# Turns of q' in the rounded 4-byte format from copies elsewhere in SBUF, two reads of x in other places, and 128-row rest products

## The chip, the cores and the metric

One NeuronCore of one Trainium2 chip runs the whole program. The metric is the device time of one launch in microseconds (us), the median of the runs shown. Engines are named as in the profile: PE (TensorE matmul), PEld (its weight load), DVE (VectorE), ACT (ScalarE), POOL (GpSimd), SP (SyncE). SP and POOL issue nearly all DMAs.

## The reference, cut to what matters

With x of shape [1, 2048, 576], 32 heads of 18 columns, and phi(t) = where(t > 0, t + 1, exp(t)) + 1e-6:

```python
q, k, v = heads(x @ wqkv)
kv  = einsum("bhsd,bhse->bhde", phi(k), v);  z = einsum("bhsd->bhd", phi(k))
num = einsum("bhqd,bhde->bhqe", phi(q), kv)
den = einsum("bhqd,bhd->bhq", phi(q), z)[..., None] + 1e-6
a = merge_heads(num / den) @ wo                                  # linear attention
fa = einsum("bsd,ed->bse", x, dft_hid_re);  fb = einsum("bsd,ed->bse", x, dft_hid_im)
b = einsum("ts,bse->bte", dft_seq_re, fa) - einsum("ts,bse->bte", dft_seq_im, fb)
g = sigmoid((x * gate_w).sum(-1, keepdims=True))
out = g * a + (1 - g) * b
```

All of it is float32. All DFT matrices come in as inputs.

## The kernel before, in words

The 2048 rows are 16 tiles of 128 rows (`NT`), or 8 pairs of tiles. The 576 columns are 4 blocks of 128 and a rest of 64 (`REST`), and for products two halves of 288 (`HALF`). Nearly all products run on operands of the type `R` (float32r, the rounded 4-byte format; `F` is plain float32): a value is split by ACT into a rounded `hi` (`hi_of`) and by DVE into `lo` = value minus `hi` (`lo_of`), and a product is the sum of three matmuls, hi·hi, hi·lo and lo·hi.

The stages, by time in the profile:

- 5 to 64 us: k' = phi(x Wk) for all 16 tiles, kept in `acc` and split into `pk`.
- 64 to 134 us: xᵀk' (matmuls `bank<-pk,c`), from it the head blocks of kv (`kv_step`, matmuls `bank<-gt,plain` on 252, 126, 144 and 72 columns), and the sums z.
- 134 to 196 us, the q' stage: q' = phi(x Wq) tile by tile (`q_tile`), 14 matmuls for each half; the second half has two more columns that give the gate. q' is written over `acc`. Beside it `build_kv` and `build_m` form the matrix M of 576 x 576 (kv of all heads times wo), which POOL's DMAs move into place (`move_m`) and `split_m` splits into `mw`. `normalise` on DVE divides each tile of q' by its denominators, in steps of a generator called `norms`.
- 185 to 258 us, the q'M stage: for each pair of tiles, `transposed` turns the normalised q': on PE 8 transposes of 128 x 128 out of `acc` (line 826) and one of the two rests of 64 columns, which DVE had copied to `last` (line 827), all with an identity matrix `ident` as the moving operand, in plain float32. ACT and DVE split the turned tiles into `qs`. Then 28 matmuls for each tile (line 226, `bank<-mw,qs`) give the attention output; ACT scales it with the gate and POOL's DMA stores it to DRAM (`att<-acc`). The turns of pair k stand ahead of the products of tile 2k-1.
- 258 to 310 us and 485 to 537 us, the hidden stages: x times the real, then the imaginary hidden DFT matrix, by seven products of quarter blocks (Strassen and Winograd's scheme). For each of 8 row pairs (p) and seven products (k) there are six matmuls on 128 rows (`bank<-wf,xf` or `bank<-wf,xb`) and one, the rest product, on 96 rows that hold the remaining 32 columns of each quarter three times, for hi·lo, hi·hi and lo·hi (line 1012, `bank<-wf,xr`, 56 in each of the two stages). The sums of x (`xforms`, tile name `xm`; `xrest`, `xr`) and of the weights (`wm`, by `right`) are made on DVE and ACT beside the stages before, written to DRAM scratch by POOL's DMAs (class `Left`, function `right`) and read back by SP's DMAs (`load_x`, `load_w`, `load_rest`). Pairs 0 and 1 of x are used straight from SBUF in the first hidden stage, pair 7 (`seven`) is written early.
- 310 to 485 us and 537 to 716 us, the sequence stages: the sequence DFT matrices times those results, again by seven products (line 1171).

ACT, DVE and SP run in the order in which the code is written. On PE the order up to the end of the q' stage is set by a scheduler, and from the q'M stage on by the code. POOL's order is the scheduler's. SBUF is laid out by hand, by offsets such as `T_AT + 76544`: buffers share places over time, and a transfer into a place waits for the last use of what lay there. `Ring` gives a few places in turn. The tables `early` (for the q' stage) and `plan` (for the q'M stage) say at which tile a step of a generator is called.

Of the kernel before, what the change touches and what calls it, by code (L numbers as in the profile page):

```python
# [8 lines left out]
F = mybir.dt.float32  # L9
# [133 lines left out]
def kernel(  # L143
# [111 lines left out]
    ident = const([P, P], F, "ident")  # L255
    make_identity(nc, ident)
# [142 lines left out]
    xrest = scratch([NP * 96, 7 * P], "xr")  # L399
    xrest_of = xrest.rearrange("(g q j r) n -> g j r q n", g=2, q=4, j=3)  # L400
# [54 lines left out]
    def right(src, rest, order):  # L455

        main, last = scratch([P, 7, 2, 2, HALF], "wm"), scratch([96, 7, HALF], "wm")

        def load(k, start):
            c = at(start, [P, 7, 2, HALF], R, "wb")[:P if k < 2 else 96]  # L460
            r, raw = c.bitcast(F)[:, :, 1], src[k] if k < 2 else rest
            for a, b in ((slice(0, 3), slice(0, 3)), (5, 3)):
                begin_after(nc.gpsimd.dma_start(out=r[:, a], in_=raw[:, b]), done[-1])
            return c

        def piece(k, start):

            c = load(k, start)
            r = c.bitcast(F)[:, :, 1]
            yield  # L470
# [4 lines left out]
            add(r[:, 6], r[:, 4], r[:, 1], ALU.subtract)  # L475
            yield
            hi_of(c[:, :, 0], r)
            yield
            if k < 2:
                for fs in (slice(0, 4), slice(4, 7)):  # L480
                    lo_of(c[:, fs, 1], r[:, fs], c[:, fs, 0])
                    nc.gpsimd.dma_start(out=main[:, fs, k], in_=c.bitcast(F)[:, fs])
                    if fs.start == 0:
                        yield
            else:
                rows = slice(32, 64)
                lo_of(c[rows, :, 0], r[rows], c[rows, :, 0])
                yield
                nc.gpsimd.dma_start(out=last, in_=c.bitcast(F)[:, :, 0])

        return (main, last), [piece(*o) for o in order]
# [127 lines left out]
    def xg_next(lo_of=lo_of):  # L619
        if xg_raw:  # L620
# [4 lines left out]
            else:  # L625
# [4 lines left out]
                                              (2, T_AT + 76544)))  # L630
# [145 lines left out]
    def q_tile(i):  # L776
        xs = kept.pop(0) if i < KEPT else split.pop(0)
        for h in range(2):
            ps = bank()[:, :QH[h]]
            run(ps, steps(xs, lambda j: wqt.row(h, j)))  # L780
# [10 lines left out]
    def normalise(k):  # L791
# [10 lines left out]
        for i in range(2):  # L802
# [4 lines left out]
            if i == 1:  # L807
                lasts.append(at(last_ring.next(), [P, 2, REST], F, "last"))
                nc.vector.tensor_copy(out=lasts[-1], in_=acc_pairs[k][:, :, KC * P:])
            yield  # L810

    lasts, last_ring = [], Ring(T_AT + 92672, 2 * REST * 4, 3)
# [5 lines left out]
    def transposed(k):  # L818

        both = [at(qs_ring.next(), [P, 9, P], R, "qs") for _ in range(2)]  # L820
        mains = [bank(), bank()]
        last = bank()[:, :P]
        for i in range(2):
            for c in range(KC):
                cs = slice(c * P, (c + 1) * P)
                nc.tensor.transpose(mains[i][:, cs], acc[2 * k + i][:, cs], ident)  # L826
        nc.tensor.transpose(last, lasts.pop(0).rearrange("p a b -> p (a b)"), ident)  # L827
# [3 lines left out]
        for i, t in enumerate(both):  # L831
            mine, other = ((slice(0, REST), slice(REST, P))[j] for j in (i, 1 - i))
            hi_of(t[mine, 8], last[mine])
            lo_of(t[other, 8], last[mine], t[mine, 8])
        return both
# [56 lines left out]
    def split_m(h):  # L892
        hi_of(mhi[:, :KC, h], mraw[:, :, h])
        lo_of(mlo[:, :, h], mraw[:, :, h], mhi[:, :KC, h])
        hi_of(mhi[:, KC, h], mrest[:, h])
# [15 lines left out]
    for f in wo_split:  # L911
        f()
    kv_step(4)
    q_tile(1)
    build_kv()
# [7 lines left out]
    early = {4: [(norms, 2)], 5: [(norms, 1), (wr_pieces[2], 1)],  # L923
             6: [(norms, 1)], 7: [(wr_pieces[2], 1)],
             8: [(wr_pieces[2], 1), (norms, 1)], 9: [(wr_pieces[2], 1), ("seven", 1)],
             10: [("seven", 1)], 11: [(wr_pieces[2], 1)],
             12: [(wr_pieces[2], 1), ("seven", 1)], 14: [("seven", 1), (norms, 1)],
             15: [("seven", 1), (norms, 1)]}
    for i in range(4, NT):
        for part in early.get(i, ()) if i > 12 else ():  # L930
            go(seven if part[0] == "seven" else part[0], part[1])
        q_tile(i)
# [5 lines left out]
        for part in early.get(i, ()) if i < 13 else ():  # L938
            go(seven if part[0] == "seven" else part[0], part[1])
        if i == NT - 3:  # L940
            queue = transposed(0)
        if i in (10, 11):
            split_m(i - 10)
# [26 lines left out]
    class Hidden:  # L970
# [4 lines left out]
        def load_w(self, k):  # L975
# [6 lines left out]
            nc.sync.dma_start(out=rl.bitcast(F)[:96], in_=self.last[:, f])  # L982
            self.w[k] = wl, rl

        def load_rest(self, p):

            self.rest[p] = at(self.lay.rest(p), [P, 7, P], R, "xr")
            n = min(NP * 96 - p * 96, P)
            nc.sync.dma_start(out=self.rest[p].bitcast(F)[:n], in_=xrest[p * 96:p * 96 + n])
# [140 lines left out]
    def sequence(m, g, src, dst, last=None, between=None):  # L1130
# [97 lines left out]
        3: [(0, 1)], 4: [(0, 1)], 5: [(0, 1)], 6: [(0, 1)], 7: [(0, 1)],  # L1228
        11: [(1, 1)], 12: [(1, 1)], 13: [(1, 1)], 14: [(1, 2)],
    }  # L1230
    paced.enter_context(tc.manual_schedule(engines={mybir.EngineType.PE}))
    for i in range(NT):
# [22 lines left out]
        for p, j in ((1, 8), (2, 11), (3, 15)):  # L1255
# [16 lines left out]
    def late(n):  # L1272
# [15 lines left out]
        if n == 31:  # L1288
            second.load_pair(2)
            second.load_rest(2)  # L1290
            second.load_rest(4)
            second.load_pair(3)
            second.load_rest(3)
            mi.load(0)
# [100 lines left out]
```

## Time and profile before

| | us |
|---|---|
| median of 3 runs | 717.15 (716.99 to 717.18) |
| the profiled execution: device time | 717.38 |
| its span, first to last instruction | 715.7 |
| PE busy | 711.6 |
| DVE busy | 601.1 |
| ACT busy | 338.5 |
| POOL busy | 54.9 |

The profiled execution has 1.7 us outside its span. The granted clock of TensorE is 1.0 over the whole run. In the groups of instructions a row reads: line, engine, operation, what is written and read, shapes and count, busy time in us, mean ns of one. The mean ns of a matmul counts from its start to the end of its drain, and matmuls overlap; what one costs in a row of its kind is read from the chain of waits instead, where pieces of one line stand one behind the other in order of time (start, us, line, count).

### The profile page before, as it was taken

The numbers are of one execution on the slowest core, as the hardware profiler recorded it, in microseconds if no ns is written. First come the engines' busy times: TensorE is split into PE (matmuls) and PEld (weight loads), VectorE is DVE, ScalarE is ACT, GpSimd is POOL, SyncE is SP. The second block draws the span as 40 slices with busy tenths as digits, with TensorE's granted clock in tenths as the row PEclk, the third lists the DMA queues.
The fourth block names the chain that finished last, engine by engine and source line by source line (L and its number), as shares of the span: only waits on it lengthen the run. The fifth ranks groups of instructions, "written<-read, shape, count | busy, mean of one in ns | idle before, by whom it ended". The sixth has DMA issues, their size and how long they took to land.

```text
span 715.7 us, 13965 instructions
## 1 busy us (share of the span) xinstructions
PE 711.6 (99%) x5436; PEld 711.1 (99%) x5436; DVE 601.1 (84%) x1020; ACT 338.5 (47%) x587; POOL 54.9 (8%) x94
## 2 busy tenths in 40 slices
PE   9999999999999999999999999999999999999998
PEld 9999999999999999999999999999999999999998
DVE  5699977687999748989999999857889988888885
ACT  5998445677644444553534334323535433343331
POOL 1112200050131110000010000000000000000000
PEclk9999999999999999999999999999999999999999
DMA  7388896874594589753475675789973544454530
GB/s 259 105 280 312 318 303 209 301 213 129 180 368 183 195 307 366 237 184 118 150 257 184 212 254 208 278 312 402 377 260 94 184 132 144 127 181 155 179 131 34
DMA packets 57525, 157.84 MB, mean 221 GB/s; under 512 B 6388, under 2 KB 15668, under 8 KB 56436
## 3 DMA queue, kind: packets, MB, share of 16 engines
q1 hardware_dynamic: 48404, 118.44, 48.9%
q0 software_dynamic: 8768, 38.12, 14.7%
q8 instruction: 43, 0.70, 0.4%
q10 hardware_dynamic: 288, 0.39, 0.2%
q14 instruction: 22, 0.18, 0.1%
HBM read 114.06 MB, written 41.39 MB: 217 GB/s over the span
## 4 chain that ended last, share of the span: by engine, by line
PE 99%; DVE 0%; issue 0%
PE bank L1171 49%; PE bank L226 23%; PE bank L1012 14%; PE bank L725 8%; PE bank L558 2%; PE bank L826 1%; PE bank L252 1%; PE bank L704 0%; PE bank L707 0%; PE bank L827 0%; DVE row L1188 0%
## 5 line engine op out<-in xcount | busy, mean ns | idle before, releaser
L1171 PE MATMUL bank<-fh,c 128*128 128x288 f32 x1792 | 350.7, 293 | 0.0
L1171 PEld LDWEIGHTS bank<-fh,c 128*128 128x128 f32 x1792 | 285.1, 188 | 0.0
L1171 PE MATMUL bank<-fl,c 128*128 128x288 f32 x896 | 262.3, 293 | 0.0
L196 ACT ACTIVATE c<-craw 128x768 fp32r<-128x768 f32 (+2 forms) x148 | 126.9, 900 | 163.6 <-DVE craw L216 154.0
L1171 PEld LDWEIGHTS bank<-fl,c 128*128 128x128 f32 x896 | 168.2, 188 | 0.0
L206 DVE TENSOR_TENSOR c<-craw,c 128x768 fp32r<-128x768 f32 (+3 forms) x148 | 146.1, 1024 | 0.8 <-ACT c L196 0.8
L226 PE MATMUL bank<-wd,xs 128*128 128x288 f32 (+1 forms) x784 | 104.9, 294 | 0.0
L226 PEld LDWEIGHTS bank<-wd,xs 128*128 128x128 f32 x784 | 103.5, 188 | 0.0
L1012 PE MATMUL bank<-wf,xf 128*128 128x288 f32 x588 | 90.8, 294 | 0.0
L1012 PEld LDWEIGHTS bank<-wf,xf 128*128 128x128 f32 x588 | 83.3, 189 | 0.0
L226 PE MATMUL bank<-mw,qs 128*128 128x288 f32 x448 | 60.7, 295 | 0.0
L725 PE MATMUL bank<-pk,c 128*128 128x288 f32 x448 | 60.0, 294 | 0.0
L725 PEld LDWEIGHTS bank<-pk,c 128*128 128x128 f32 x448 | 59.1, 188 | 0.0
L226 PEld LDWEIGHTS bank<-mw,qs 128*128 128x128 f32 x448 | 59.0, 188 | 0.0
L216 DVE TENSOR_TENSOR craw<-craw,craw 128x256 f32<-128x256 f32 x128 | 54.4, 425 | 5.1
L216 DVE TENSOR_TENSOR ys<-bank,ys 128x288 f32<-128x288 f32 x63 | 28.8, 457 | 28.2 <-PE bank L1171 25.7
L216 DVE TENSOR_TENSOR craw<-craw 128x512 f32<-128x512 f32 x64 | 43.9, 687 | 7.6 <-PE bank L1171 3.7
L196 ACT ACTIVATE fh<-fl 128x864 fp32r<-128x864 f32 (+1 forms) x36 | 30.3, 868 | 28.0 <-DVE fl L216 20.0
L395 DVE SCALAR_TENSOR_TENSOR acc<-bank,e 128x288 f32<-128x288 f32 x64 | 28.6, 454 | 16.5 <-ACT e L394 16.3
L206 DVE TENSOR_TENSOR fl<-fl,fh 128x864 fp32r<-128x864 f32 (+1 forms) x36 | 35.4, 988 | 1.6
L1012 PE MATMUL bank<-wf,xr 96*128 96x288 f32 x112 | 33.3, 298 | 0.0
L216 DVE TENSOR_TENSOR fl<-bank,y 128x288 f32<-128x288 f32 x48 | 21.8, 454 | 11.1 <-PE bank L1012 9.6
(106 smaller groups left out, 662.1 us busy)
## 6 DMA issues: line engine op xcount, KB each, us to landing
xf<-xm SPq DMA_DIRECT2D x42, 512.0 KB, 9.2
craw<-in_cr_dram SPq DMA_DIRECT2D x32, 512.0 KB, 3.9
craw<-in_ci_dram SPq DMA_DIRECT2D x32, 512.0 KB, 3.7
xm<-xb POOLq DMA_DIRECT2D x8, 1024.0 KB, 6.6
wf<-wm SPq DMA_DIRECT2D x14, 576.0 KB, 6.4
xraw<-in_xa_dram SPq DMA_DIRECT2D x25, 320.0 KB, 3.5
xr<-xr SPq DMA_DIRECT2D x14, 448.0 KB, 8.5
xm<-xb POOLq DMA_DIRECT2D x8, 768.0 KB, 8.2
```

What stands on the lines that cost most here:

```text
L196: return nc.scalar.activation(dst, src, AF.Copy, bias=bias)
L206: nc.vector.tensor_tensor(out=dst, in0=src, in1=hi, op=ALU.subtract)
L216: nc.vector.tensor_tensor(out=dst, in0=a, in1=b, op=op)
L226: nc.tensor.matmul(ps, a, b, start=(n == 0), stop=(n == len(pairs) - 1))
L252: nc.tensor.matmul(warm[:, :136], unit[:, :P], unit, start=True, stop=True)
L395: nc.vector.scalar_tensor_tensor(dst, ps, 0.0, e, op0=ALU.max, op1=ALU.add)
L558: nc.tensor.matmul(ps[i][h], x[:, i_x * P:(i_x + 1) * P], wkt.row(h, j), start=(c == 0 and n == 0), stop=(c == KC and n == 1))
L725: nc.tensor.matmul(ps[h][:, :HALF], t[:, a, k], pk[s][:, b, half(h)], start=(s == 0 and n == 0), stop=(s == NT - 1 and n == len(turn) - 1))
L826: nc.tensor.transpose(mains[i][:, cs], acc[2 * k + i][:, cs], ident)
L1012: nc.tensor.matmul(ps, a, b, start=(start and n == 0), stop=(n == len(ops) - 1), skip_group_check=True)
L1171: nc.tensor.matmul(ps[q], c[x][l > 2][:, l - 3 * (l > 2), k], factors[p](y, f), start=(p == 0 and i == 0), stop=(p == NP - 1 and i == 2))
```

## The change

Seven things change.

1. `ident` is now in the type `R`: POOL builds it in plain float32 as `unit_f`, and one ACT instruction copies it. The normalised pair of q' is copied by two POOL DMAs, bit by bit, from `acc` and `last` to one of three buffers `turn` of type `R` (`move_normal`), and `turn` transposes out of these instead of `acc`. Number and shape of the transposes stay: 72 of 128 x 128.
2. `norms` and the small pieces are called at other tiles (`early`, `plan`): the normalisation of pairs 3 to 7 ends one tile sooner than before, that of pair 1 two, that of pair 2 six.
3. `q_tile` opens both halves at once: 9 matmuls of the first half, 9 of the second, then 5 and 5. The turns of pair 0 stand between the 9s and the 5s of tile 13. PE follows the written order from tile 2 of the q' stage on.
4. The last 32 rows of the rest products are filled with zeros: `last` of the weights and `xr` have 128 rows, and a rest product is a matmul on 128 rows. `rest_piece` makes the rest of the weights on 64 partitions of half the width, with a zeroed third part (POOL's memset) and 8 DMAs to DRAM instead of one, and zeros behind the last pair of `xrest`.
5. The rest piece of the weights lies at `T_AT + 84672` instead of `T_AT + 76544`, `last` at `T_AT + 63232`. Pair 2 of x is read into `T_AT + 65536` to `T_AT + 79872`.
6. Pair 2 of x is read at tile 0 of the q'M stage instead of 3, pair 3 at tiles 9 to 12, one piece at a time, instead of 15. Before the second hidden stage the rest of pair 4 is read behind pair 3 instead of ahead of it.
7. `split_m` is cut into `m_hi` (tiles 9 and 10) and `m_lo` (tiles 10 and 11).

```diff
-    ident = const([P, P], F, "ident")
-    make_identity(nc, ident)
+    unit_f = at(SLOT_AT + P * 4, [P, P], F, "unit_f")
+    make_identity(nc, unit_f)
+    ident = const([P, P], R, "ident")
+    nc.scalar.activation(ident, unit_f, AF.Copy)
...
-    xrest = scratch([NP * 96, 7 * P], "xr")
+    xrest = scratch([NP * 96 + 32, 7 * P], "xr")
...
-        main, last = scratch([P, 7, 2, 2, HALF], "wm"), scratch([96, 7, HALF], "wm")
+        main, last = scratch([P, 7, 2, 2, HALF], "wm"), scratch([P, 7, HALF], "wm")
...
+        def rest_piece(start):
+            c = at(start, [2 * 32, 3, 7, HALF // 2], R, "wb")
+            f = c.bitcast(F)
+            r = f[:, 1]
+            load(r, rest)
+            nc.gpsimd.memset(f[:, 2], 0.0)
+            yield
+            for _ in sums(r):
+                pass
+            yield
+            hi_of(c[:, 0], r)
+            yield
+            lo_of(c[:, 1], r, c[:, 0])
+            for k, a in enumerate((0, 1, 0, 2)):
+                for q in range(2):
+                    ps, cs = slice(q * 32, q * 32 + 32), slice(q * HALF // 2, (q + 1) * HALF // 2)
+                    nc.gpsimd.dma_start(out=last[k * 32:k * 32 + 32, :, cs], in_=f[ps, a])
...
     wr_forms, wr_pieces = right(wr, wr_rest, ((0, ACC_AT + 6144), (1, T_AT + 113664),
-                                              (2, T_AT + 76544)))
+                                              (2, T_AT + 84672)))
...
-    def q_tile(i):
+    def q_tile(i, between=iter(())):
...
+        both = [bank()[:, :QH[h]] for h in range(2)]
+        todo = [list(steps(xs, lambda j, h=h: wqt.row(h, j))) for h in range(2)]
+        for part in (slice(0, 9), slice(9, 14)):
+            for h in range(2):
+                for n in range(part.start, part.stop):
+                    nc.tensor.matmul(both[h], *todo[h][n], start=(n == 0), stop=(n == 13))
+            if part.start == 0:
+                next(between, None)
...
+    def move_normal():
+        while normal:
+            k, last = normal.pop(0)
+            o = turn_ring.next()
+            main = at(o, [P, 2, KC * P], R, "turn")
+            rest = at(o + 2 * KC * P * 4, [P, 2, REST], R, "turn")
+            nc.gpsimd.dma_start(out=main.bitcast(F), in_=acc_pairs[k][:, :, :KC * P])
+            nc.gpsimd.dma_start(out=rest.bitcast(F), in_=last)
+            moved.append((main, rest))
...
-                nc.tensor.transpose(mains[i][:, cs], acc[2 * k + i][:, cs], ident)
-        nc.tensor.transpose(last, lasts.pop(0).rearrange("p a b -> p (a b)"), ident)
+                nc.tensor.transpose(mains[i][:, cs].bitcast(R), main[:, i, cs], ident)
+        nc.tensor.transpose(last.bitcast(R), rest.rearrange("p a b -> p (a b)"), ident)
+        yield
...
-    early = {4: [(norms, 2)], 5: [(norms, 1), (wr_pieces[2], 1)],
...
+    early = {4: [(norms, 2), (wr_pieces[2], 1)], 5: [(norms, 1)],
...
+        move_normal()
         if i == NT - 3:
-            queue = transposed(0)
+            go(turning)
...
-            nc.sync.dma_start(out=rl.bitcast(F)[:96], in_=self.last[:, f])
+            nc.sync.dma_start(out=rl.bitcast(F), in_=self.last[:, f])
...
-            ops.append((self.rest[p][:96, 6 - k], wl[:96]))
+            ops.append((self.rest[p][:, 6 - k], wl))
...
-        3: [(0, 1)], 4: [(0, 1)], 5: [(0, 1)], 6: [(0, 1)], 7: [(0, 1)],
+        2: [(0, 1)], 3: [(0, 1)], 5: [(0, 1)], 10: [(0, 1)], 11: [(0, 1), (1, 1)],
...
-        go(norms, 1 if i in (4, 6) else 2)
+        go(norms, 1 if i in (2, 4) else 2)
         for k, n in plan.get(i, ()):
             go(made[k], n)
+        move_normal()
...
-        if i == 3:
+        if i == 0:
             hidden.load_pair(2)
-        if i == 15:
-            hidden.load_pair(3)
+        for k, j in ((0, 9), (2, 10), (4, 11), (6, 12)):
+            if i == j:
+                hidden.load_x(3, k)
```

How the order of instructions moves at the places that the prediction speaks of. On PE, at tile 13 of the q' stage (`wd` is a half of Wq, `xs` a tile of x, split; `acc_87` is pair 0 of q'), before:

```order
L226 MATMUL bank<-wd_1308,xs_2303 128x290
L226 MATMUL bank<-wd_1307,xs_2303 128x290
L826 MATMUL bank<-ident_76,acc_87 128x128 x4
L226 MATMUL bank<-wd_1424,xs_2303 128x288 x5
L226 MATMUL bank<-wd_1307,xs_2303 128x290 x5
L826 MATMUL bank<-ident_76,acc_87 128x128 x4
L827 MATMUL bank<-ident_76,last_2043 128x128
L226 MATMUL bank<-wd_1424,xs_2350 128x288
```

The same place now (line 803 is in `q_tile`, 868 and 869 in `turn`):

```order
L803 MATMUL bank<-wd_1309,xs_2334 128x290
L868 MATMUL bank<-ident_81,turn_2057 128x128 x8
L869 MATMUL bank<-ident_81,turn_2058 128x128
L803 MATMUL bank<-wd_1426,xs_2334 128x288 x5
L803 MATMUL bank<-wd_1309,xs_2334 128x290 x5
L803 MATMUL bank<-wd_1426,xs_2385 128x288
```

The nine transposes stand together and read `turn`, no longer `acc`. In the q'M stage they stand at the same places as before.

On POOL, tiles 0 to 4 of the q'M stage, before (`att` is the store of a tile's attention output, `xb` the quarters of x pairs 0 and 1 read in):

```order
L1241 DMA att_2620<-acc_87 128x576
L411 DMA xb_2665<-in_xq_dram 128x2x256 x2
L1241 DMA att_2621<-acc_87 128x576
L1241 DMA att_2622<-acc_88 128x576
L1241 DMA att_2623<-acc_88 128x576
L411 DMA xb_2834<-in_xq_dram 128x2x256 x2
L1241 DMA att_2608<-acc_89 128x576
```

The same place now:

```order
L1297 DMA att_2651<-acc_89 128x576
L413 DMA xb_2695<-in_xq_dram 128x2x256 x2
L1297 DMA att_2652<-acc_89 128x576
L850 DMA turn_2768<-acc_92 128x2x512
L851 DMA turn_2769<-last_2766 128x128
L1297 DMA att_2653<-acc_90 128x576
L1297 DMA att_2654<-acc_90 128x576
L413 DMA xb_2874<-in_xq_dram 128x2x256 x2
L1297 DMA att_2639<-acc_91 128x576
L850 DMA turn_2914<-acc_93 128x2x512
L851 DMA turn_2915<-last_2912 128x128
```

The copies of pair 3 (`acc_92`) stand behind the store of tile 1, and those of pair 4 (`acc_93`) behind the store of tile 4; pairs 5, 6 and 7 follow behind tiles 6, 8 and 10. The copies of pairs 0 to 2 are issued in the q' stage.

On SP, the reads of x pair 3 for the first hidden stage, before (`xm_98` is pair 3; `wf` are weights, `xr` rests of x):

```order
L981 DMA wf_3412<-wm_359 128x4x288
L982 DMA wf_3413<-wm_360 96x288
L989 DMA xr_3449<-xr_103 128x896
L995 DMA xf_3451<-xm_98 128x1024
L995 DMA xf_3453<-xm_98 128x1024
L995 DMA xf_3455<-xm_98 128x1024
L995 DMA xf_3457<-xm_98 128x512
L989 DMA xr_3479<-xr_103 128x896
```

And now (`xm_100` is pair 3):

```order
L1052 DMA xf_3212<-xm_100 128x1024
L1039 DMA wf_3259<-wm_361 128x4x288
L1040 DMA wf_3260<-wm_362 128x288
L1052 DMA xf_3263<-xm_100 128x1024
L1052 DMA xf_3324<-xm_100 128x1024
L1039 DMA wf_3361<-wm_361 128x4x288
L1040 DMA wf_3362<-wm_362 128x288
L1052 DMA xf_3365<-xm_100 128x512
```

The four reads of pair 3 stand between the reads of weights, ahead of the last one. The reads of pair 2 stand right behind the last tile of x for q' both before and now; what differs for them is the place they are written to, which the rest piece of the weights no longer overlaps.

More of the change, by code (lines that the diff above doesn't have):

```diff
@@ L475, in piece @@
             add(r[:, 6], r[:, 4], r[:, 1], ALU.subtract)
+        def piece(k, start):
+            c = at(start, [P, 7, 2, HALF], R, "wb")
+            r = c.bitcast(F)[:, :, 1]
+            load(r, src[k])
+            yield
+            yield from sums(r)
             yield
@@ L834, in transposed @@
             lo_of(t[other, 8], last[mine], t[mine, 8])
+    def transposed(k):
+        both = []
+        for _ in turn(k, both):
+            pass
         return both
@@ L931 @@
             go(seven if part[0] == "seven" else part[0], part[1])
-        q_tile(i)
+        if i == NT - 3:
+            queue = []
+            turning = turn(0, queue)
+            q_tile(i, turning)
+        else:
+            q_tile(i)
         build_m({4: (2, 3), 5: (4,)}.get(i, ()))
```

85 lines of the change are left out of this document (41 added, 44 removed).

## The prediction

> **What bounds the kernel now.** I read the totals first, then the chain that ended last, then PE's waits, then PE's groups by shape. Totals and chain, from the page:
>
> ```profile
> PE 711.6 (99%) x5436; PEld 711.1 (99%) x5436; DVE 601.1 (84%) x1020; ACT 338.5 (47%) x587; POOL 54.9 (8%) x94
> PE 99%; DVE 0%; issue 0%
> PE bank L1171 49%; PE bank L226 23%; PE bank L1012 14%; PE bank L725 8%; PE bank L558 2%; PE bank L826 1%; PE bank L252 1%; PE bank L704 0%; PE bank L707 0%; PE bank L827 0%; DVE row L1188 0%
> ```
>
> The waits of PE, one row in all (waited for: us, times, longest):
>
> ```profile
> PE bank L252 <- PEq L1382: 0.8, 1, 0.8
> ```
>
> PE waits once, 0.8 us, at the very start. From there to the end its instructions are the chain, one behind the other. So the kernel gets shorter only where an instruction on PE gets shorter or goes, and longer where PE meets a wait that it does not have today. Everything else in this change (DVE, ACT, POOL, SP, DMA) counts by the second of these alone.
>
> Now what the touched instructions cost. The chain of waits in order of time (start, us, line, count), first where rounded matmuls of 252 and 126 (then 144 and 72) columns alternate in `kv_step`, then where turns stand among the products of q'M:
>
> ```profile
> 134.01 0.11 PE bank L704
> 134.12 0.06 PE bank L707
> 134.18 0.17 PE bank L704
> 134.35 0.06 PE bank L707
> 134.41 0.07 PE bank L704
> 134.48 0.04 PE bank L707
> ...
> 196.50 0.87 PE bank L826 x8
> 197.38 0.11 PE bank L827
> ...
> 205.75 7.34 PE bank L226 x56
> ...
> 221.42 0.87 PE bank L826 x8
> ```
>
> Eight transposes take 0.87 us, 109 ns each, and the ninth 0.11. A product of 288 columns takes 7.34 / 56 = 131 ns. So 128 columns in plain float32 cost 0.85 ns a column, 288 rounded ones 0.45. A rounded matmul of 126 columns (line 707) holds the chain for 0.06 us; but with its neighbour of 252 columns it is 0.17 + 0.06 = 0.23 us, 0.115 for each of two weight loads.
>
> The groups by shape, matmuls and then weight loads (count | busy, mean ns):
>
> ```profile
> L1012 PE MATMUL bank<-wf,xf 128*128 128x288 f32 x588 | 90.8, 294 | 0.0
> L1012 PE MATMUL bank<-wf,xr 96*128 96x288 f32 x112 | 33.3, 298 | 0.0
> L826 PE MATMUL bank<-ident,acc 128*128 128x128 f32 x64 | 8.4, 272 | 0.0
> L827 PE MATMUL bank<-ident,last 128*128 128x128 f32 x8 | 2.2, 273 | 0.0
> L226 PEld LDWEIGHTS bank<-mw,qs 128*128 128x128 f32 x448 | 59.0, 188 | 0.0
> L826 PEld LDWEIGHTS bank<-ident,acc 128*128 128x128 f32 x64 | 7.5, 140 | 0.0
> L707 PEld LDWEIGHTS bank<-gt,plain 128*126 128x126 f32 x20 | 3.8, 189 | 0.0
> L704 PEld LDWEIGHTS bank<-gt,plain 128*72 128x72 f32 x5 | 0.7, 141 | 0.0
> ```
>
> The last two columns of mean times matter. A rest product on 96 rows lasts 298 ns, its neighbours on 128 rows 294. A rounded weight load of 126 or 128 columns lasts 188 or 189 ns, one of 72 columns 141; the load of a transpose, though it has 128 columns, lasts 140.
>
> **The turns.** Before: 64 x 0.109 + 8 x 0.11 = 7.9 us. No row shows a rounded transpose. From below the bound is the shortest rounded matmul, 72 columns in 0.04 us: 72 x 0.04 = 2.9 us, a gain of 5.0. From above it is the rounded weight load that binds in `kv_step`, 0.115 us: 72 x 0.115 = 8.3 us, a loss of 0.4. I take 0.06, the row of line 707, as nearest in type and width: 72 x 0.06 = 4.3 us, a gain of 3.6. The reason to take it rather than 0.115 is the weight load: in a turn it already lasts 140 ns instead of 188, as short as a rounded one of 72 columns, and two of those with their matmuls take 0.07 + 0.04 = 0.11 us, 0.055 each. So if the turn's load keeps that length, 0.055 to 0.06 is what both load and columns give.
>
> Here a rule of the Trainium skill speaks against the change. "TensorE: Matmul & The Clock Gate", section "LDWEIGHTS (loading the stationary operand)", gives a weight load's time as its columns over 1.2, so 107 ns for 128 columns, however many rows it has; by it a turn stays at 107 ns, and the estimate is 72 x 0.107 = 7.7 us, a gain of 0.2 instead of 3.6. The alternating row above (0.115 for a load of 126 columns) agrees with it, the shorter load of the transposes does not.
>
> **The rest products.** 112 of them, each 298 - 294 = 4 ns longer than its neighbours: 112 x 4 = 0.45 us gained if 128 rows cost what they cost there. Bounds: nothing, or 0.45. I take 0.45, since the shape becomes that of the neighbours exactly. The reads of weights grow from 96 to 128 rows on SP's queue, off PE's path.
>
> **The copies of q'.** 16 DMAs on POOL's queue, of 512 and 64 KB a pair, and PE now waits for them. Pairs 0 to 2 are copied many tiles ahead. Pair 3 has three tiles, pairs 4 to 7 two tiles between copy and turn. The timeline of POOL shows when the store ahead of pair 4's copies is issued:
>
> ```profile
> 214.04 0.56 POOL L1241 DMA_DIRECT2D att<-acc  x1 [1.57 <-ACT acc L1239]
> ```
>
> What transfers of that queue take, from the DMA issues between 213 and 247 us (count, KB each, median us to landing):
>
> ```profile
> att<-acc POOLq DMA_DIRECT2D x8, 288.0 KB, 2.8
> ...
> xm<-xb POOLq DMA_DIRECT2D x1, 1024.0 KB, 5.9
> xm<-xb POOLq DMA_DIRECT2D x1, 768.0 KB, 3.9
> ```
>
> And from those between 185 and 258.4 us:
>
> ```profile
> xm<-xb POOLq DMA_DIRECT2D x3, 768.0 KB, 9.2
> ```
>
> The copy is issued at about 214.04 + 0.56 = 214.6 and its turn stands at 221.42, or 221.0 once the turn between is 0.4 us shorter: 6.4 us. For 576 KB I go by the quiet rows, between 2.8 for 288 KB and 3.9 for 768: about 3.5 us. That leaves 2.9 us, so I cost the copies at nothing. What hides them is the products of two tiles, 7.34 us; if that cover fails, each us of lateness is a us of PE, up to four times.
>
> DVE must also have normalised the pair by then. Busy times by stretch (PE, PEld, DVE, ACT, POOL, then granted clock, DMA share, GB/s):
>
> ```profile
> 160.00:185.00 25.00, 25.00 (x192) 25.00 (x191) 20.98 (x37) 20.83 (x46) 2.31 (x3) 1.00 0.37 113
> 197.00:213.50 16.50, 16.50 (x132) 16.50 (x131) 15.26 (x30) 7.19 (x18) 5.11 (x8) 1.00 1.02 378
> 213.50:230.00 16.50, 16.50 (x131) 16.50 (x130) 15.14 (x27) 8.49 (x19) 2.74 (x5) 1.00 0.54 197
> ```
>
> DVE has 1.2 to 1.4 us free of 16.5. The change moves work on it between tiles and adds none, and the normalisation ends one tile sooner, which is the tile that the copy takes back.
>
> **The moved reads and the rest.** SP's timeline, last tiles of x for q' and the reads that follow:
>
> ```profile
> 173.32 4.04 SPq L283 DMA_DIRECT2D xraw<-in_xa_dram  x2
> 188.23 1.75 SPq L995 DMA_DIRECT2D xf<-xm  x4
> ...
> 255.92 3.83 SPq L995 DMA_DIRECT2D xf<-xm  x4
> ```
>
> Today pair 2 waits from 177.4 to 188.2 us for the rest piece of the weights, which lies in its place, and then falls into the stretch where the DMA engines are full (share 1.02). With the new places it can start at about 177, in a stretch with a share of 0.37. Pair 3's four reads move from 256 us into the gaps of tiles 9 to 12, behind weights, and ahead of the last weights. PE waits for none of these today, so nothing is gained on its path: 0. They make room for the 4.6 MB of copies.
>
> The ACT copy of `ident` stands ahead of the first split of the weights. ACT's timeline there:
>
> ```profile
> 2.53 0.31 ACT L258 ACTIVATE ones<-ones_f 128x128 fp32r<-128x128 f32 x1
> 4.12 0.44 ACT L196 ACTIVATE wd<-wraw 128x288 fp32r<-128x288 f32 x1 [1.28 <-DMA wraw<-in_wk_dram]
> ```
>
> ACT sits idle for 1.28 us there; another 0.3 us fits: 0. The interleaved halves of `q_tile` are the same 28 matmuls with two banks open instead of one: 0, at most the 0.8 us of one bursting split in the last tile. The rest piece halves the width of its DVE work and adds a memset and 7 DMAs on POOL, which is 8% busy: 0.
>
> **The sum**, against the profiled execution: 717.38 us, of which 715.7 is span and 1.7 lies around it. Span after: 715.7 - 3.6 - 0.45 = 711.65; time 713.3. The median of the runs stands 0.23 below that execution, so 713.1; I say 713.2.
>
> **The rivals.**
>
> *The weight load binds the turn.* For it: 0.115 us for each load in `kv_step`, and rounded loads of 128 columns last 188 ns everywhere. Against it: the turn's load lasts 140. Then a turn costs 0.109 to 0.115, and the rest products are all that is left: 717.15 - 0.45 + (0 to 0.4) = 716.7 to 717.1, within what a measurement here can tell from no change (0.2%, 1.4 us). The rule of the Trainium skill named above would give the same. Chance 0.23.
>
> *The copies land late.* The other side. For it: the row of 768 KB between 185 and 258 us, 9.2 us; with it each of four copies misses its turn by 9.2 - 6.4 = 2.8 us, 11.2 in all: 713.2 + 11.2 = 724.4. Against it: pair 2's reads leave just that stretch, and after 213 us the same transfers take 3.9 and 5.9. It decides slower from 713.2 + 4 x L = 718.6, where L = 1.35 us, so from a landing of 7.75 us. Chance 0.14: 0.09 past that point (718.6 to 724), 0.05 short of it (714 to 718).
>
> *A turn is bound by neither and costs between,* 0.08 us: 717.15 - 2.1 - 0.45 = 714.6. Chance 0.06; the rest, 0.57, is the forecast, with its own range of 711.7 (0.04 us a turn) to 714.2 (0.5 us of small waits and no gain from the rest products).
>
> **How the numbers follow.** Faster by over 0.2%: 0.57 + 0.06 and a little of the late copies, 0.65. Within 0.2%: 0.23 and the rest of the small delays, 0.25. Slower: 0.10. The range runs from 711.7 to 717.4, so that the rival of the weight load with 0.3 us of small waits lies in it; what is left out is late copies past 717.4 and a turn below 0.04 us.
>
> **What would show it.** Right: in the chain of waits nine transposes together take about 0.5 us instead of 0.98; PE has no wait but the first; the group of rest products reads 294 ns. The forecast falls if the transposes keep 109 ns or more; if PE's waits name a DMA of `turn` at one of pairs 4 to 7 (PE would then sit between the products of two tiles); or if at the start of the first hidden stage PE waits for `wf`, whose reads wait for the stores `att` that now share POOL's queue with the copies.

## The result, and the profile after

The changed kernel is slower: 720.87 us (median of 6 runs, 720.69 to 723.44) against 717.16 (6 runs, 716.42 to 717.35), ratio over all runs 1.0063, 95% interval 1.0051 to 1.0074. The forecast was 713.2 with a range up to 717.4. The execution in the profile took 723.44 us, 2.6 more than the median.

The totals of the page, and its chain:

```profile
PE 713.0 (99%) x5436; PEld 712.2 (99%) x5436; DVE 597.3 (83%) x1020; ACT 336.6 (47%) x588; POOL 75.2 (10%) x127
PE 91%; issue 5%; POOL 2%; DMA 1%; DVE 0%; POOLq 0%
```

Before, the chain was PE to 99%. Now POOL, a DMA and issue time stand in it. PE's waits name the DMA (us in all, times, longest); the one other wait, 0.9 us, is that of the start, as before:

```profile
PE bank L868 <- DMA turn<-acc: 4.7, 2, 2.4
```

PE's timeline around them (start, us until the last one has drained, instruction, count, and in brackets the idle time before). Line 868 is the turns, line 226 the products of q'M:

```profile
221.07 0.80 PE L868 MATMUL bank<-ident,turn 128*128 128x128 f32 x8
...
221.78 7.52 PE L226 MATMUL bank<-mw,qs 128*128 128x288 f32 x56
231.53 1.21 PE L868 MATMUL bank<-ident,turn 128*128 128x128 f32 x8 [2.22 <-DMA turn<-acc]
...
232.66 8.62 PE L226 MATMUL bank<-mw,qs 128*128 128x288 f32 x56
241.12 0.80 PE L868 MATMUL bank<-ident,turn 128*128 128x128 f32 x8
...
251.80 1.10 PE L868 MATMUL bank<-ident,turn 128*128 128x128 f32 x8 [2.43 <-DMA turn<-acc]
```

The waits stand ahead of the turns of pairs 5 and 7. A second loss follows each: the 56 products behind pair 5's turn take 8.62 us, those behind pair 4's 7.52, and the turns take longer too. The busy times by stretch tell why (PE, PEld, DVE, ACT, POOL, then granted clock, DMA share, GB/s):

```profile
231.50:235.00 3.50, 3.48 (x19) 3.48 (x20) 1.73 (x4) 1.59 (x4) 0.75 (x2) 0.52 0.63 237
235.10:240.00 4.90, 4.90 (x40) 4.90 (x39) 4.70 (x9) 1.50 (x3) 0.55 (x1) 1.00 0.09 35
251.80:255.50 3.70, 3.70 (x20) 3.70 (x21) 1.87 (x4) 1.53 (x4) 0.00 (x0) 0.54 1.01 420
```

For about 3.4 us behind each wait TensorE is granted half its clock. Where nothing waits, a pair (turns and 56 products) takes about 8.1 us in the rounded format (the chain of e7, below, shows it). Here pairs 4 and 5 together take 241.12 - 221.07 = 20.05 us, and pair 6 with the wait ahead of pair 7 takes 251.80 - 241.12 = 10.68. So the waits cost 2.3 and 2.6 us, and the half clock behind them 1.5 and 1.6 (the last from 251.80 to the first hidden stage: 13.43 us, against 11.82 in e7, which doesn't wait). Together 8 us in this execution.

Why the copies are late: the chain's piece of pair 7's copy, and the two copies on POOL's timeline:

```profile
242.95 8.80 DMA turn<-acc
```

```profile
222.85 0.72 POOL L850 DMA_DIRECT2D turn<-acc  x1
...
242.95 0.73 POOL L850 DMA_DIRECT2D turn<-acc  x1 [0.17 <-issue]
```

SP's timeline there. Line 1052 reads pair 3 of x:

```profile
222.03 0.43 SPq L1052 DMA_DIRECT2D xf<-xm  x1
241.07 0.37 SPq L1039 DMA_DIRECT2D wf<-wm  x1
241.49 0.50 SPq L1040 DMA_DIRECT2D wf<-wm  x1
242.10 0.85 SPq L1052 DMA_DIRECT2D xf<-xm  x2
```

Each time reads of pair 3 are issued within 1 us ahead of the copy. The copy of pair 7 takes 8.8 us to land; it would have to land in about 6.4 (251.80 less the wait of 2.43, less 242.95). The row of the five copies issued between 196 and 262 us (count, KB each, median us to landing) shows what they take otherwise:

```profile
turn<-acc POOLq DMA_DIRECT2D x5, 512.0 KB, 3.4
```

Those of pairs 3, 4 and 6, with no such read just ahead of them, land in 3.1, 3.3 and 3.4 us, near the 3.5 that was forecast for all.

What was meant to get shorter did. Pair 0's turns in the chain, and the group of rest products:

```profile
183.62 0.64 PE bank L868 x8
184.26 0.08 PE bank L869
```

```profile
L1069 PE MATMUL bank<-wf,xr 128*128 128x288 f32 x112 | 32.9, 294 | 0.0
```

A turn takes 80 ns instead of 109, a rest product 294 instead of 298.

### The profile page after: what moved, and what is told of

It reads as the page before. It is cut to its first block, busy times and chain, and to the rows that moved or that the text cites. A ratio compares the mean times of both kernels' runs of the same rounds, so it can differ in the third digit from the quotient of the medians.

```text
span 721.7 us, 14042 instructions
## 1 busy us (share of the span) xinstructions
PE 713.0 (99%) x5436; PEld 712.2 (99%) x5436; DVE 597.3 (83%) x1020; ACT 336.6 (47%) x588; POOL 75.2 (10%) x127
## 4 chain that ended last, share of the span: by engine, by line
PE 91%; issue 5%; POOL 2%; DMA 1%; DVE 0%; POOLq 0%
PE bank L1228 49%; PE bank L1069 14%; PE bank L226 8%; PE bank L745 8%; PE bank L803 8%; PE bank L578 2%; DMA turn<-acc 1%; POOL att L1297 1%; PE bank L252 1%; PE bank L724 0%; POOL xb L413 0%; POOL turn L850 0%; POOL turn L851 0%; PE bank L868 0%; PE bank L727 0%
## 5 line engine op out<-in xcount | busy, mean ns | idle before, releaser
L226 PE MATMUL bank<-mw,qs 128*128 128x288 f32 x448 | 62.6, 301 | 0.0
L226 PEld LDWEIGHTS bank<-mw,qs 128*128 128x128 f32 x448 | 61.1, 195 | 0.0
L803 PE MATMUL bank<-wd,xs 128*128 128x288 f32 (+1 forms) x448 | 60.9, 296 | 0.0
L226 PE MATMUL bank<-wd,xs 128*128 128x288 f32 x336 | 44.2, 293 | 0.0
```

What stands on the lines that cost most here:

```text
L226: nc.tensor.matmul(ps, a, b, start=(n == 0), stop=(n == len(pairs) - 1))
L803: nc.tensor.matmul(both[h], *todo[h][n], start=(n == 0), stop=(n == 13))
```

## The experiments

Ratios are to the kernel before on the same chip, with 95% intervals.

| run | what | us (runs) | ratio |
|---|---|---|---|
| e1_pair3_late | pair 3 read at tile 15, as before | 715.19 (10) | 0.9976 [0.9967, 0.9985] |
| e2_plain_turns | plain turns, no copies | 720.04 (6) | 1.0047 [1.0034, 1.0059] |
| e3_dve_writes | rounded turns, written by DVE, no copies | 719.34 (7) | 1.0033 [1.0021, 1.0045] |
| e4_turn_forms | other turns in three pairs | 726.32 (1) | - |
| e5_pair3_early | three reads of pair 3 earlier | 715.26 (7) | 0.9972 [0.9961, 0.9983] |
| e6_plain_late | e2, pair 3 at tile 15 | 716.95 (11) | 1.0000 [0.9991, 1.0009] |
| e7_dve_late | e3, pair 3 at tile 15 | 715.20 (8) | 0.9974 [0.9964, 0.9984] |
| e8_reads_alone | before, pair 3 at tiles 9 to 12 | 717.13 (11) | 1.0000 [0.9992, 1.0009] |
| e9_pair0_early | changed, stores of pair 0 as before | 722.55 (6) | 1.0070 [1.0052, 1.0088] |
| e10_plain_pair0_early | e2, stores of pair 0 as before | 716.75 (11) | 0.9995 [0.9986, 1.0003] |
| e11_warm_pe | changed, idle transposes in the waits | 720.49 (5) | 1.0050 [1.0037, 1.0063] |
| e12_changed_again | the changed kernel | 723.84 (1) | - |

**The reads of pair 3 put back (e1).**

```diff
-        for k, j in ((0, 9), (2, 10), (4, 11), (6, 12)):
-            if i == j:
-                hidden.load_x(3, k)
+        if i == 15:
+            hidden.load_pair(3)
```

> The four reads of x pair 3 go back to tile 15 of the q'M stage; all else is as in the changed kernel. Theory (the copies of q' lose the DMA engines to these reads, which start within 2 us of the copies of pairs 5 and 7): pair 5's copy loses one 512 KB neighbour, pair 7's two; at the 370 GB/s that the stretch moved that is 1.4 and 2.8 us. Waits of PE for turn fall from 2.2 + 2.4 us to about 0.8 + 0, no drop of PE's clock or one, time 715.5 to 717.5. Rival (the copies stand behind stores on POOL's own queue, the reads don't matter): both waits stay near 2.3 us, time 720 to 721 as for the changed kernel.

715.19 us, 5.7 less than the changed kernel. PE's waits, and the DMA issues from 240 to 252 us of this kernel (count, KB each, median us to landing):

```profile
PE bank L252 <- PEq L1440: 0.9, 1, 0.9
```

```profile
xm<-xb POOLq DMA_DIRECT2D x1, 1024.0 KB, 6.7
att<-acc POOLq DMA_DIRECT2D x3, 288.0 KB, 3.9
...
turn<-acc POOLq DMA_DIRECT2D x1, 512.0 KB, 5.4
```

The same rows of the changed kernel:

```profile
xm<-xb POOLq DMA_DIRECT2D x1, 1024.0 KB, 10.2
att<-acc POOLq DMA_DIRECT2D x3, 288.0 KB, 7.6
...
turn<-acc POOLq DMA_DIRECT2D x1, 512.0 KB, 8.8
```

With the reads away the copy lands in 5.4 us instead of 8.8, in time, and the other transfers of the stretch are shorter too. Moving these four reads takes the whole loss away and leaves the kernel 0.24% faster than before. The theory had the cause right and expected more to be left (0.8 us of wait, 715.5 or more). The cover stays thin: reads of weights still stand ahead of the copies of pairs 5 and 7, and pair 5's lands in 6.1 us, with 6.3 between its issue and its turn.

**Without the copies (e2, e3).** e2 keeps everything but the rounded turns: float32 from `acc` and `last`, nothing copied. In e3 the last step of `normalise` writes the pair straight into `turn`, rounded, for which some steps of `norms` are called later in the q' stage; e3 (and e7, below) so leaves out what rounding takes from q', its `lo`.

```diff
 e2
-    ident = const([P, P], R, "ident")
+    ident = const([P, P], F, "ident")
...
-            moved.append((main, rest))
+            moved.append((acc_pairs[k], last))
...
 e3
-            nc.vector.scalar_tensor_tensor(a, a, EPS,
+            if i == 0:
+                t = at(turn_ring.next(), [P, 2, D], R, "turn")
+            b = t[:, i].rearrange("p (h d) -> p h d", d=DH)
+            nc.vector.scalar_tensor_tensor(b, a, EPS,
```

> Turns in plain float32 straight out of acc again, no copies and no wait for them; all other parts of the change stay (128-row rest products, both halves interleaved, reads and small pieces in their new places). Theory (all of the loss is the copies): no wait of PE but the first, a turn 109 ns, rest products 0.8 us shorter, time 716.2 to 716.8. Rival (another part costs time too, such as the interleaved halves or the moved reads): 717.5 or more, with no wait for turn.

> The copies by DMA go: DVE's normalisation writes the pair straight into turn in the rounded format (so q' is rounded before its turn, which leaves its lo part out), and last is copied into that format by DVE; the early steps of norms stand one to four tiles later in the q' stage. Theory (rounded turns take 80 ns, copies and their two clock drops cost 8 us of the profiled execution): no wait, 8 x 0.26 = 2.1 us from the turns and 0.8 from the rest products, time 714.0 to 714.8. Rival (what is lost beside the copies is as large as the gain): 716.5 or more. Rival (a turn of 80 ns only after the wait of a copy): the chain shows 109 ns a turn and 716.4.

Both are slower than before, though there is no copy to wait for: 720.04 and 719.34. In both the theory fell and the rival came that something else costs time too. PE's waits and the chain of e2:

```profile
PE bank L1064 <- DMA wf<-wm: 2.0, 1, 2.0
```

```profile
251.62 4.58 DMA att<-acc
...
256.32 9.04 DMA wf<-wm
```

The last weights of the first hidden stage lie where the attention output lay, so their read waits for its store, and then takes 9.04 us itself. Behind this wait too the clock is halved (windows of e2):

```profile
266.80:270.50 3.70, 3.70 (x18) 3.70 (x18) 1.87 (x3) 1.18 (x3) 0.00 (x0) 0.54 0.59 201
```

e3 waits 1.7 us at the same stage, in the profiled execution, which was its fastest (717.34). Its row on PE's timeline, SP's row for the last weights, and the median landing of such reads issued between 250 and 264 us:

```profile
263.89 1.02 PE L1066 MATMUL bank<-wf,xb 128*128 128x288 f32 x6 [1.66 <-DVE fl L216]
```

```profile
255.42 0.37 SPq L1036 DMA_DIRECT2D wf<-wm  x1
```

```profile
wf<-wm SPq DMA_DIRECT2D x1, 576.0 KB, 8.3
```

The row names DVE, but 255.42 + 8.3 is 263.7, just before PE goes on; and in e7 below, the same DVE instructions end at 263.3 and PE has long begun this product, at 261.56. I read this wait as the weights'. So the copies are one victim of the moved reads; without copies there is another.

**Turns in other forms (e4).** Pair 1 turned by an ordinary rounded product with the identity, pair 2 by transposes of 96 and 32 rows, pair 3 in plain float32:

```diff
+                if k == 1:
+                    nc.tensor.matmul(mains[i][:, cs], main[:, i, cs], ident, start=True, stop=True)
+                elif k == 2:
+                    for rs in (slice(0, 96), slice(96, P)):
+                        o = slice(c * P + rs.start, c * P + rs.stop)
+                        nc.tensor.transpose(mains[i][:, o].bitcast(R), main[rs, i, cs], ident[rs, rs])
+                elif k == 3:
+                    nc.tensor.transpose(mains[i][:, cs], acc[2 * k + i][:, cs], unit_f2)
```

> As the changed kernel, but pair 1 is multiplied with the identity as an ordinary rounded product (not a transpose; q' is rounded), pair 2 is turned in parts of 96 and 32 rows, pair 3 in plain float32 out of acc; pairs 0 and 4 to 7 as in the changed kernel (control, 80 ns a turn). Theory A (the moving columns set a turn: plain float32 moves at half the rate): pair 3 about 109 ns, pair 1 about 80, pair 2's 96 + 32 together near 80 to 100. Theory B (the weight load sets a rounded turn at 80 ns, as a transpose loads faster than a product): pair 1 about 110 to 115, pair 2 about 2 x 80 = 160 for both parts. My step that took 60 ns from a row of kv_step is wrong under both.

PE's timeline and the weight loads by shape (line 879 is the ordinary turn, 871 the product, 875 the cut one):

```profile
196.59 1.01 PE L871 MATMUL bank<-ident,turn 128*128 128x128 f32 x8
197.43 0.25 PE L880 MATMUL bank<-ident,turn 128*128 128x128 f32 x1
...
204.87 2.88 PE L875 MATMUL bank<-ident,turn 96*128 96x96 f32 x16
207.68 0.28 PE L880 MATMUL bank<-ident,turn 128*128 128x128 f32 x1
```

```profile
L879 PEld LDWEIGHTS bank<-ident,turn 128*128 128x128 f32 x40 | 4.1, 146 | 3.3 <-DMA turn<-acc 3.3
...
L871 PEld LDWEIGHTS bank<-ident,turn 128*128 128x128 f32 x8 | 1.0, 191 | 0.0
```

The product costs (197.43 - 196.59) / 8 = 105 ns against 80 for the transpose; its load lasts 191 ns against 146. So a transpose's load is shorter than an ordinary rounded one of the same shape, as the prediction argued, and the turn is shorter with it. The load alone doesn't set the time: pair 3's plain turns have loads of 141 ns and start 0.11 us apart, as before the change. Two smaller transposes cost (207.68 - 204.87) / 8 = 351 ns in the place of 80, so a turn's time is not its rows or columns alone; why a cut one is that dear stays open. Theory A is right for pair 3 alone, theory B near for pair 1 alone, and neither for pair 2.

**Pair 3 earlier, and the versions without a wait (e5 to e8).** e5 reads three parts of pair 3 right behind pair 2 and the fourth at tile 15, and keeps the copies. e6 and e7 are e2 and e3 with the edit of e1. e8 is the kernel before with the reads alone moved:

```diff
 e5
-        for k, j in ((0, 9), (2, 10), (4, 11), (6, 12)):
-            if i == j:
-                hidden.load_x(3, k)
+            for k in (0, 4, 6):
+                hidden.load_x(3, k)
+        if i == 15:
+            hidden.load_x(3, 2)
 e8, in the kernel before
-        if i == 15:
-            hidden.load_pair(3)
+        for k, j in ((0, 9), (2, 10), (4, 11), (6, 12)):
+            if i == j:
+                hidden.load_x(3, k)
```

> The reads of x pair 3 leave tiles 9 to 12: three of the four (1.25 MB) stand right behind pair 2's at the end of the q' stage, the fourth at tile 15. The copies of q' stay. Theory (what costs is that the reads share the DMA engines with the copies and with the last weights, from 220 to 257 us; the reads alone cost nothing): no wait of PE but the first, time 714.3 to 715.3, as with the late reads or a little less, since the first hidden stage then has 1.25 MB less to move at its start. Rival (the reads cost PE time wherever they stand, or delay the first weights and the copy of pair 3): 716 or more, with a wait between 190 and 215 us.

> Plain float32 turns out of acc, no copies, and the reads of pair 3 back at tile 15; the rest of the change stays. Theory (in the run with plain turns and the reads at tiles 9 to 12 the loss was the wait for the last weights, held up by those reads): no wait, time 716.1 to 716.8, that is the kernel before less 0.8 us of rest products. Rival (the later small pieces of pair 0, whose stores now fall at 240 to 245 us, hold the weights up by themselves): a wait for wf at the first hidden stage stays, 718 or more.

> DVE writes the pair in the rounded format, without copies (q' is rounded before its turn, its lo part left out), and the reads of pair 3 are back at tile 15. Against the kernel with late reads and copies it shows what the copies still cost; against the one with plain turns and late reads, what a rounded turn is worth. Theory: no wait, 714.0 to 714.8, so 2.1 below the plain turns; copies that are in time cost 0 to 0.8 us. Rival (the copies cost PE nothing once they are in time and the missing 1 us is elsewhere): the same time as with the copies, 715.2.

> The kernel before with one part of the change alone: the four reads of pair 3 at tiles 9 to 12 instead of 15. Theory (the moved reads delay the stores that the weights wait for, and the weights themselves): a wait for wf at the first hidden stage of 0.5 to 2 us, or none if the stores of pair 0, which stand earlier here, leave room; time 717 to 719. Rival (the reads do harm only beside copies or the later stores of pair 0): no wait, 716.6 to 717.2. Rival of my prediction (they help): below 716.

None of the four has a wait of PE but the first. Copied in time (e1 715.19, e5 715.26) or written by DVE (e7 715.20) is the same, so that the rival of e7 came and not its theory: in time, a copy costs nothing that shows. e6, 0.15 us above its expected range, against e7 gives the worth of the turns: 716.95 - 715.20 = 1.75 us. The two also differ in who writes `turn` and in the tiles of some steps of `norms`, none of which PE waits for. Their chains, e6 first:

```profile
213.23 0.87 PE bank L863 x8
214.10 0.11 PE bank L864
214.21 7.34 PE bank L226 x56
```

```profile
211.94 0.64 PE bank L865 x8
212.58 0.09 PE bank L866
212.67 7.42 PE bank L226 x56
220.09 0.64 PE bank L865 x8
```

The nine turns take 0.73 us instead of 0.98, but the 56 products behind them take 7.42 (7.36 behind the next turns) instead of 7.34. A pair takes 8.15 (the next 8.08) instead of 8.32. So of 8 x 0.25 = 2.0 us some 0.3 is given back by the products behind the turns, which agrees with the 1.75. e8 shows that the reads at tiles 9 to 12 alone do no harm to the kernel before: 717.13 against 717.09 on the same chip, with no wait, as its first rival had it.

**Who else is needed (e9, e10).** e2 is slower than e8, and both read pair 3 at these tiles. Among what else differs is that the change stores the sums of pair 0 later (`plan`). Both runs put that table back:

```diff
-        2: [(0, 1)], 3: [(0, 1)], 5: [(0, 1)], 10: [(0, 1)], 11: [(0, 1), (1, 1)],
-        12: [(1, 1)], 13: [(1, 1)], 14: [(1, 2)],
+        3: [(0, 1)], 4: [(0, 1)], 5: [(0, 1)], 6: [(0, 1)], 7: [(0, 1)],
+        11: [(1, 1)], 12: [(1, 1)], 13: [(1, 1)], 14: [(1, 2)],
```

> The changed kernel with one table put back: the pieces of x pair 0 (forms and stores, `plan`) are called at tiles 3 to 7 of the q'M stage again instead of 2 to 11, so that its last stores leave POOL's queue before the reads of pair 3. Theory A (what holds up the copies of pairs 5 and 7 is the reads of pair 3 at tiles 9 to 12, together with whatever else moves; the later stores of pair 0 weigh at the second place only): PE still waits about 2 us ahead of pair 5's turns, the wait ahead of pair 7's shrinks below 1.5 us or goes; 717 to 719 us. Rival B (the stores of pair 0, moved later, are the party that the reads of pair 3 cannot stand beside): both waits go, about 715.2. Rival C (the place of these stores does not matter): both waits and about 720.9.

> The kernel with plain float32 turns and no copies that took 720.0 us, with the pieces of x pair 0 back at tiles 3 to 7 and the reads of pair 3 still at tiles 9 to 12: nearly the order of transfers of the kernel before with these reads alone moved, which took 717.1. Theory A (without copies it is the later stores of pair 0, beside the reads of pair 3, that make the last weights late at the start of the first hidden stage): no wait of PE but the first, 716.9 to 717.2. Rival B (the weights or other shifted transfers are late whatever pair 0's stores do): PE waits 2 us for `wf` as it did, about 720.

My theory A of e9 fell, rival C came: 722.55 us, and PE's waits on the copies as before,

```profile
PE bank L868 <- DMA turn<-acc: 4.7, 2, 2.8
```

so the copies are late beside the reads of pair 3 wherever pair 0's stores stand. In e10 theory A held: 716.75 us and no wait but the first. Without copies the reads of pair 3 do harm only together with the later stores of pair 0. Two pairs of transfers that are harmless one by one collide: reads and copies at pairs 5 and 7, and behind them reads and stores at the last weights.

**Work in the place of the wait (e11).**

```diff
+        if k in (5, 7):
+            for n in range(24):
+                cs = slice(n % 4 * P, n % 4 * P + P)
+                nc.tensor.transpose(mains[n // 4 % 2][:, cs].bitcast(R), ident, ident)
```

> The changed kernel with 24 idle transposes (identity by identity, 128 x 128, written to the banks that the real ones overwrite) ahead of the turns of pairs 5 and 7: about 2.0 us of work, at 85 ns each, in the place of waits of 2.2 and 2.4 us. It leaves nothing out and adds this work. Theory A (the half clock of 3.4 us that follows each wait comes from PE having stood still): waits of 0.2 to 0.5 us remain, no stretch at half clock, and the kernel gains 1.7 us at each of two places, 720.9 - 3.4 = 717.5. Rival B (the clock drops for another reason at these times): the stretches at half clock stay, about 720.9. Rival C (PE's own work ahead of the turns delays the buffers behind it): slower than 720.9.

PE's timeline, with the 56 products behind the first place and the idle transposes at the second, and its waits:

```profile
231.44 7.51 PE L226 MATMUL bank<-mw,qs 128*128 128x288 f32 x56
...
246.88 2.18 PE L868 MATMUL bank<-ident 128*128 128x128 f32 x24
```

```profile
PE bank L1073 <- DMA wf<-wm: 0.9, 1, 0.9
...
PE bank L872 <- DMA turn<-acc: 0.2, 1, 0.2
```

The 56 products take 7.51 us again, not 8.62: no half clock in the whole execution (mean 1.0), though PE did nothing useful in that time. From the first products of q'M to those of the first hidden stage it takes 68.74 us, against 72.03 in the profile of the changed kernel: 3.3 less, as theory A says. But the first hidden stage now starts sooner, meets the last weights on the way (0.9 us) and gives 1.1 back. The rest of the 2.95 us between the two profiled executions, 0.75, lies ahead of the q' stage (it starts at 134.18 us here, at 134.93 there) and does not come from the edit. The median, 720.49, is 0.4 below the changed kernel's 720.87; 717.5, which I expected, started from the median. Four of the six executions behind it show a mean clock of 0.998 to 0.999, so I think they had one halved stretch, not two. e12 was to show such an execution:

> The changed kernel unaltered, one more profiled execution. Four of its six runs took 720.7 to 720.9 us at a mean clock of 0.998 to 0.999, the two others 723.2 and 723.4 at 0.995, and only one of the latter has been seen in a profile. Theory A (waits and clock are tied together: a mean of 0.998 is one stretch of 3.4 us at half clock instead of two): an execution near 720.8 has one wait of 2 us or more with a half clock behind it, and one shorter wait with none. Rival B (the shorter runs have copies in time at one of the two places): one wait and one stretch only. If the execution is one of 723, it repeats the two waits of 2.2 and 2.4 us and decides nothing.

It took 723.84 us, with waits of 2.1 and 2.5 us at the same two places, and decides nothing. What the shorter executions look like stays open.

## Why the prediction was wrong

- **The copies of q'** is the step that failed: "That leaves 2.9 us, so I cost the copies at nothing." The 3.5 us came from rows of the kernel before, from a stretch into which the change itself brings more traffic. Measured: 8.7 us (231.53 - 222.85) and 8.8 against a window of about 6.4. The issue at two tiles' distance and the window were right, and so was the 3.5 us where no read of pair 3 stands ahead (3.1 to 3.4 us for pairs 3, 4 and 6).
- **The moved reads** failed with it: "PE waits for none of these today, so nothing is gained on its path: 0. They make room for the 4.6 MB of copies." I asked who waits for the moved reads, and not what waits beside them. They took the room of pairs 5 and 7 (e1, e5: without them no wait). And where the copies are gone, they and the moved stores of pair 0 delay the last weights (e2 against e10); that `wf` could be late was named as a sign, but with no price.
- **The rival "the copies land late"** is what happened, with its point of 7.75 us passed by both. Its mechanism was half right: not four copies by 2.8 us each but two by 2.3 and 2.6, and through pair 3's reads instead of pair 2's. Its price missed the half clock, 1.5 to 1.6 us behind each wait in this profile (e11: without standing still, none). Its chance of 0.14 leaned on "after 213 us the same transfers take 3.9 and 5.9", the same row of the old traffic.
- **The turns** were mis-sized: 0.06 us was taken, 0.080 measured, and the products behind them give some back; 1.75 us instead of 3.6 (e6, e7). The row of line 707 that I took stands between matmuls of 252 columns and holds the chain for less than its own load of 189 ns lasts; it says nothing of nine loads in a row. The second reason, "if the turn's load keeps that length, 0.055 to 0.06 is what both load and columns give", fell too: the load kept it (median 141 ns), and the turn takes 80. The third rival, 0.08 us, had the size; its 714.6 is what e1, e5 and e7 come near to with 715.2. The Trainium skill's 107 ns for a weight load, "TensorE: Matmul & The Clock Gate", section "LDWEIGHTS (loading the stationary operand)", did not bind the turn. The Trainium skill, same page, section "Back-to-back issue gap", gives about 81 ns for a matmul of 128 columns in a stream of loads and matmuls, and the 80 ns here agree; the 105 ns of e4's product do not.
- **The rest products**: 4 ns each, as forecast. In the traces the two hidden stages of e6 take 103.04 us against 103.61; in the time of e6 against before (716.95, 717.09) that is below what can be told.
- **The rest** (order of halves, `ident`, rest piece of the weights): 0, as forecast. q' and q'M together take 131.04 us in e6 and 130.92 before.

The sum: of the 7.7 us between 713.2 and 720.87, 5.7 is the reads of pair 3 (e1) and 1.9 the turns (3.6 less 1.75); 0.1 is left. The runs come from several chips, on which the kernel before took 716.87 to 717.50, so tenths of this sum can't be read.

## What to carry to other kernels

A transfer that now must land in time is priced with the traffic of the kernel after, its own edits included: list what each queue issues in the two microseconds ahead of it. When one engine is the whole chain, a read that nobody waits for still costs once it goes ahead of a transfer that somebody waits for; moving it to tile 15, or most of it to tile 0, was worth 5.7 us here and made the change a gain (e1 or e5, 715.2 us). And price a short instruction from a row of its own kind in sequence, not from one that stands between long neighbours.

## What the hardware showed that was not expected

A wait of PE of about 2 us cost more than itself here. Behind waits of 1.82 (e4), 2.0 (e2), 2.2 and 2.4 us the granted clock fell to one half for about 3.4 us; behind 1.04 (e4) and 1.66 (e3) it did not. PE's timeline of e4 with its two waits, its window behind the second, and its window behind the cut transposes of pair 2, ahead of which PE did not wait:

```profile
234.35 0.87 PE L879 MATMUL bank<-ident,turn 128*128 128x128 f32 x8 [1.04 <-DMA turn<-acc]
...
252.56 1.16 PE L879 MATMUL bank<-ident,turn 128*128 128x128 f32 x8 [1.82 <-DMA turn<-acc]
```

```profile
252.00:256.00 4.00, 3.44 (x19) 3.44 (x20) 1.69 (x4) 1.53 (x4) 0.22 (x1) 0.60 1.00 420
208.00:212.00 4.00, 4.00 (x20) 4.00 (x20) 3.01 (x7) 1.38 (x4) 0.00 (x0) 0.57 0.57 188
```

The last row shows that standing still is not the only cause: behind 2.8 us of cut transposes the clock was halved for as long. Nor is it shown that the length of a wait alone decides. The two halved stretches begin 20.5 us apart in the changed kernel and in e12, and 44.4 in e4, which is 6 and 13 times 3.41, so where a wait falls may count as well; no run here separates the two.

The Trainium skill, "TensorE: Matmul & The Clock Gate", section "Part 1: The HAM clock gate (the "warmup" mystery)", describes a clock that halves after an idle window of about 3.4 us and recovers after a busy one. The length of the slow stretch agrees; the idle time that sets it off was shorter here. 24 transposes of no use kept the clock at full speed (e11), so whole transposes of 128 x 128 count as work for it here; those of 96 and 32 rows in e4 did not keep it up.
